# A slot of the second network: both first-layer products first, then the three tiles of its predecessor

## The chip, the cores and the metric

The kernel runs on one core of a Trainium2 chip. The metric is the time of one execution on the device, in microseconds (us). The engines are TensorE (PE, with its weight loads shown as PEld), VectorE (DVE), ScalarE (ACT), GpSimd (POOL) and SyncE (SP, which issues the transfers).

## The reference, cut to what matters

```python
def reference(**kwargs):
    attn_out = _attn_ref(q, k, v, p)             # packed attention, two softmaxes
    x = attn_out as 2304 tokens x 512
    x = _moe_ref(x, w_gate, w1, w2)              # eight experts, balanced gate
    return _moe2_ref(x, w_in, w_out, s, b)

def _moe2_ref(x, w_in, w_out, s, b):             # the second network
    h = x @ w_in                                 # 2304 x 512 @ 512 x 2048
    r = np.maximum(h, 0.0)
    g = s * (r * r) + b
    return (g @ w_out).astype(np.float32)        # 2304 x 2048 @ 2048 x 512
```

## The kernel before, in words

The program has three stages: attention, the experts, and the second network. Only the third is touched by the change. Every product is made of three passes (high x high, high x low, low x high), because each operand is held as a high part and a low part.

The second network goes through eight units `v` of 256 hidden columns (two halves `f` of 128), and within a unit through six blocks `b` of 384 tokens. One unit and one block make a **slot**, 48 in all. A slot has two first-layer products, here called f0 and f1 (`mm1b`, 12 matmuls of 384 columns each, L415), and three second-layer tiles t0, t1, t2 (`tile2`, 6 matmuls of 512 columns each, L390). The tiles of a slot are those of the slot before it: `coming` collects a slot's tiles, and `slot` hands them to the next slot as `ready`.

After f0 or f1 the result goes through an **epilogue**: ACT takes the positive part into `r` (L421), DVE multiplies into `g` (L422), which is the last reader of the product's PSUM bank, DVE scales and shifts `g` (L423), ACT casts it to the high part of `h` (L424), POOL subtracts to get the low part (L425). After a tile, DVE adds the PSUM bank to `acc` (L432; in unit 0 ACT copies instead, L430). In a tile, matmuls 1 to 3 read the f0 half of `h`, matmuls 4 and 5 the high part of its f1 half and matmul 6 the low part of its f1 half.

Buffers: the first-layer products share two PSUM banks (`ps_h`), the tiles three (`ps_y`). `r` is one buffer, `g` two. `h` holds three blocks.

Beside that, units 0 to 6 convert the next unit's weights from 64-bit words (`load_w64`): eight steps per unit, two per slot from block 1 on, given to `slot` as its `side` jobs. A step is seven DVE instructions (L111, L113, L114, L116, L118, L119, L120), one on ACT (L123) and one on POOL (L124). Every other step also issues a transfer of raw words on SP. The step's tiles `ex` and `m` are one buffer each, and a unit's first steps write weight buffers that the tiles of the slot before block 1 still read.

Order of the work: the attention stage is ordered by hand. After it, the framework's planner sets each engine's queue. It takes the program's order as priority and its own costs for when an instruction will be ready, so DVE's queue can hold a conversion step's instructions between those of an epilogue. Each queue is then carried out strictly in that order. The order in which a slot's jobs are written is set in `slot`:

```python
        per = [first[0]] + todo[:1] + [first[1]] + todo[1:]
        for n, job in enumerate(per):
            job()
            if side:
                side.pop(0)()
```

`first` holds f0 and f1, `todo` the predecessor's three tiles. A side job is written after each of them as long as there are any. `slot1` (the experts) and `slot2` (the second network) both call `slot`.

Of the kernel before, what the change touches and what calls it, by code (L numbers as in the profile page):

```python
# [15 lines left out]
B, H, S, HD, NPK = 4, 8, 576, 64, 32  # L16
NT, D = B * S, H * HD
E, FF1, FF2 = 8, 1024, 2048
NTT = NT // 128      # token tiles
NC = D // 128        # 128-row chunks of the model dimension  # L20
FU = 256             # hidden columns of a unit
UF = FU // 128
U1 = E * FF1 // FU   # units of the experts
UE = FF1 // FU       # units of an expert
U2 = FF2 // FU       # units of the second network
HB = S // 2          # tokens of a block of the experts: half a sequence
PT = 2 * S           # tokens of a pair of sequences
BLK = 384            # tokens of a block of the second network
NB = NT // BLK
TPB = BLK // 128  # L30
KC, NKC = 96, 6      # keys of a chunk, chunks
SCALE = 1.0 / 8.0    # 1 / sqrt(HD)
EPS = 1e-9
PASSES = ((0, 0), (0, 1), (1, 0))

# [2 lines left out]
def tile_kernel(ctx: ExitStack, tc: tile.TileContext, qT, kT, vv, pb, w1c, w2c, wcat64, wg, sv, bv, out):  # L38
# [8 lines left out]
    ps_h = pool("ps_h", 2, space=bass.MemoryType.PSUM)  # L47
    ps_m = pool("ps_m", 3, space=bass.MemoryType.PSUM)

    # chunks 0 and 1 of (high part, low part) of what the feed-forward networks read, by tokens:  # L50
    # first the second attention's weights, heads x packed keys in rows; then the experts' sum
    xa = [big.tile([128, 2, NT], F32R, name=f"xa{n}") for n in range(2)]
    xb = []
    acc = big.tile([128, NTT, D], F32, name="acc")
    h = big.tile([128, UF, 2, PT], F32R, name="h")

    ident = const.tile([128, 128], F32, name="ident")
    ones = const.tile([128, 128], F32, name="ones")
    wgr = const.tile([128, NC, E], F32, name="wgr")
    lg = const.tile([128, NTT, E], F32, name="lg")  # L60
    pm = const.tile([128, NTT, E], F32, name="pm")
    sb_ = const.tile([128, 2], F32, name="sb_")
# [6 lines left out]
    def x_part(n, c):  # L69
        return xa[n][:, c, :] if c < 2 else xb[n][:, c - 2, :]  # L70

# [1 line left out]
    wts = {}  # L73
    tmp_p = []

# [2 lines left out]
        return wts[key]  # L78

    def load_w1(u):  # L80
        # a head's rows: high parts in rows 0-63, low parts in rows 64-127
        w = w_new((1, u))
        for i in range(2):
            r = raw_p.tile([128, 1024], F32, tag="raw", name="raw")
            for n in range(2):
                nc.sync.dma_start(out=r[64 * n:64 * n + 64, :], in_=w1c[u, :, 1024 * i:1024 * i + 1024])
            yield
            A.copy(w[:, i, :], r)  # L88
            G.tensor_tensor(out=w[64:128, i, :], in0=r[64:128, :], in1=w[64:128, i, :].bitcast(F32),  # L89
                            op=ALU.subtract)  # L90
# [7 lines left out]
        G.tensor_tensor(out=w[:, 1, :], in0=r, in1=w[:, 0, :].bitcast(F32), op=ALU.subtract)  # L98

    def load_w64(key, f):  # L100
        # float64 words to float32: (mantissa + 2^20) * (sign, exponent - 20), rounded to nearest
        w = w_new(key)
        for half in range(2):
            r = raw_p.tile([128, 1024], U32, tag="raw", name="raw64")
            nc.sync.dma_start(out=r, in_=wcat64[f, :, 1024 * half:1024 * half + 1024])
            for q in range(2):
                rv = r[:, 512 * q:512 * q + 512].rearrange("p (n k) -> p n k", k=2)
                lo, hi = rv[:, :, 0], rv[:, :, 1]
                ex = tmp_p[-1].tile([128, 256], U32, tag="ex", name="ex")
                m = tmp_p[-1].tile([128, 256], F32, tag="m", name="m")  # L110
                V.tensor_scalar(out=ex, in0=hi, scalar1=20, scalar2=0x7FF,  # L111
                                op0=ALU.logical_shift_right, op1=ALU.bitwise_and)
                V.tensor_scalar(out=ex, in0=ex, scalar1=916.0, scalar2=1171.0, op0=ALU.max, op1=ALU.min)  # L113
                V.tensor_scalar(out=ex, in0=ex, scalar1=916.0, scalar2=8388608.0,  # L114
                                op0=ALU.subtract, op1=ALU.mult)
                V.scalar_tensor_tensor(out=ex, in0=hi, scalar=0x80000000, in1=ex,  # L116
                                       op0=ALU.bitwise_and, op1=ALU.bitwise_or)
                V.tensor_scalar(out=hi, in0=hi, scalar1=0xFFFFF, scalar2=None, op0=ALU.bitwise_and)  # L118
                V.scalar_tensor_tensor(out=m, in0=lo, scalar=2.0 ** -32, in1=hi, op0=ALU.mult, op1=ALU.add)  # L119
                V.scalar_tensor_tensor(out=m, in0=m, scalar=2.0 ** 20, in1=ex.bitcast(F32),  # L120
                                       op0=ALU.add, op1=ALU.mult)
                o = slice(512 * half + 256 * q, 512 * half + 256 * q + 256)
                A.copy(w[:, 0, o], m)  # L123
                G.tensor_tensor(out=w[:, 1, o], in0=m, in1=w[:, 0, o].bitcast(F32), op=ALU.subtract)  # L124
                yield

# [1 line left out]
    NG = B * 2  # L128
    at = {}

# [3 lines left out]
    accf = acc.rearrange("p t d -> p (t d)")  # L134

    def spare(o, n):
        # rows of acc, which the experts reach after the attention
        return accf[:, o:o + n]

    def a_load(g):  # L140
# [64 lines left out]
        at[g]["w"] = w  # L205

    def ppt(g):
        # a head's packed values, transposed, in rows 0-63 and again in rows 64-127
        b, i = divmod(g, 2)
        p_ = psa("h", "ps_p")  # L210
        nc.tensor.transpose(p_[:, :128], at[g].pop("w").rearrange("p a d -> p (a d)"), ident)
        pv = p_[:, :128].rearrange("p (c j n) -> p c j n", c=2, j=2)
        for j in range(2):
            r, o = slice(64 * j, 64 * j + 64), NPK * (j ^ (b & 1))
            A.copy(ppf[r, b, 2 * i:2 * i + 2, o:o + NPK], pv[r, :, j, :])
        s_ = [p_[:, NPK * n:NPK * n + NPK] for n in range(4)]
        o = [[pp[:, i, n, k, b ^ n, :] for n in range(4)] for k in range(2)]
        for n in range(4):
            A.copy(o[0][n], s_[n])  # L219
        for n in range(4):  # L220
            V.tensor_tensor(out=o[1][n], in0=s_[n], in1=o[0][n].bitcast(F32), op=ALU.subtract)
# [38 lines left out]
        A.copy(xa[0][o], a2T)  # L260
        G.tensor_tensor(out=xa[1][o], in0=a2T, in1=xa[0][o].bitcast(F32), op=ALU.subtract)

    # (stage, waves after the group's first)
    STAGES = ((sub2, 5), (norm2, 6), (s1, 0), (a1t, 1), (exp1, 0), (exp2, 5), (a2t, 7), (a2x, 7), (av, 2),
              (s2, 4), (ppt, 3))

# [2 lines left out]
            if 0 <= w - lag < NG:  # L269
                stage(w - lag)  # L270

# [1 line left out]
    def balance(mid):  # L273
        wgz = mid.tile([128, B, 2, 128], F32R, tag="wgz", name="wgz")
        G.memset(wgz.bitcast(F32), 0.0)
# [58 lines left out]
            V.scalar_tensor_tensor(out=pm, in0=pm, scalar=float(NT // E),  # L334
                                   in1=c[:, 2].to_broadcast([128, NTT, E]), op0=ALU.mult, op1=ALU.mult)

# [1 line left out]
    zs = {}  # L338

    def zmm(u, n, p_=None):  # L340
        # rows of a head in a sequence: block (head ^ sequence) of 32, so that blocks stay where they are
        i, k = divmod(n, 2)
        if n == 0:
            for pr in range(2):
                zs[u, pr] = z_p.tile([128, 2, 2, 2, FU], F32R, tag="z", name="z")
        w = wts[1, u].rearrange("p a m -> p (a m)")
        p_ = psm("ps_z") if p_ is None else p_
        for j in range(2):
            m = 2 * k + j
            for a in range(2):  # L350
                mmul(p_[:, j * FU:(j + 1) * FU], pp[:, i, m, a].rearrange("p q n -> p (q n)"),  # L351
                     w[:, (4 * i + m) * FU:(4 * i + m + 1) * FU], start=(a == 0), stop=(a == 1))
        return p_
# [50 lines left out]
                                       op0=ALU.mult, op1=ALU.add)  # L404
        return put

# [1 line left out]
    def mm1b(v, b, f):  # L408
        w = wts[3, v, f]
        p_ = ps_h.tile([128, 512], F32, tag="h", name="ps_1")  # L410
# [31 lines left out]
        A.copy(xh, p_[:, :BLK])  # L442
        V.tensor_tensor(out=xl, in0=p_[:, :BLK], in1=xh.bitcast(F32), op=ALU.subtract)

# [1 line left out]
    order = [(u, pr) for u in range(U1) for pr in range(2)]  # L446
    ready, coming = [], []

    def slot(first, side=()):
        # the products of a block, among them what earlier blocks made ready  # L450
        side = list(side)
        todo = ready[:]
        del ready[:]
        per = [first[0]] + todo[:1] + [first[1]] + todo[1:]
        for n, job in enumerate(per):
            job()
            if side:
                side.pop(0)()
        for s_ in side:
            s_()  # L460
        ready.extend(coming)
        del coming[:]
# [9 lines left out]
    def slot2(v, b, side=()):  # L472
        first = [lambda f=f: mm1b(v, b, f) for f in range(UF)]
        ws = [[wts[3, v, f][:, k, D:2 * D] for k in range(2)] for f in range(UF)]
        for t in range(TPB):
            coming.append(lambda t=t: tile2(ws, (b % 3) * BLK + t * 128, b * TPB + t, put2(v)))
        slot(first, side)

    def side1(x, q):
        jobs = []  # L480
# [14 lines left out]
    with tc.tile_pool(name="early", bufs=1) as early:  # L495
        pp = early.tile([128, 2, 4, 2, B, NPK], F32R, name="pp")
        ppf = early.tile([128, B, NC, 2 * NPK], F32, name="ppf")
        with tc.manual_schedule(), tc.tile_pool(name="at", bufs=1) as at_p:
# [26 lines left out]
            for q in range(4):  # L525
                side = [lambda: wave(NG + 3 + q), lambda: next(loads, None)]
# [6 lines left out]
        with tc.tile_pool(name="mid", bufs=1) as mid:  # L533
# [3 lines left out]
            for x in range(1, len(order) - 1):  # L537
                for q in range(4):
                    side = side1(x, q)
# [17 lines left out]
    with tc.tile_pool(name="late", bufs=1) as late:  # L557
        tmp_p.append(late)
        xb += [late.tile([128, 2, NT], F32R, name=f"xb{n}") for n in range(2)]
        x = len(order) - 1  # L560
        for q in range(4):
            slot1(x, q, [lambda b=q - 1, c=c: flip(b, c) for c in range(NC)] if q else ())
        for v in range(U2):
            conv = None
            for b in range(NB):
                side = []
# [53 lines left out]
```

## Time and profile before

| what | value |
| --- | --- |
| median of 3 runs | 1840.36 us (1840.31 to 1841.12) |
| span of the profiled execution, first to last instruction | 1839.9 us |
| time beyond the span, by the median | 0.5 us |
| PE busy, of the span | 1761.9 us (96%) |
| DVE busy, of the span | 1399.3 us (76%) |
| mean granted TensorE clock | 0.990 |
| second network, first product to the last instruction | 1396.3 to 1839.9 us |

The profiled execution has no time of its own apart from its span; the span and the median of the runs differ by 0.5 us. A share of the whole span is a mean over stages that differ, so the second network has to be read slot by slot. In the rows, `[0.80 <-ACT h L424]` means that the engine was idle for 0.80 us before the instruction and that the write of `h` by ACT at line 424 ended the idle time.

### The profile page before, as it was taken

The numbers are of one execution on the slowest core, as the hardware profiler recorded it, in microseconds if no ns is written. First come the engines' busy times: TensorE is split into PE (matmuls) and PEld (weight loads), VectorE is DVE, ScalarE is ACT, GpSimd is POOL, SyncE is SP. The second block draws the span as 40 slices with busy tenths as digits, with TensorE's granted clock in tenths as the row PEclk, the third lists the DMA queues.
The fourth block names the chain that finished last, engine by engine and source line by source line (L and its number), as shares of the span: only waits on it lengthen the run. The fifth ranks groups of instructions, "written<-read, shape, count | busy, mean of one in ns | idle before, by whom it ended". The sixth has DMA issues, their size and how long they took to land.

```text
span 1839.9 us, 26426 instructions
## 1 busy us (share of the span) xinstructions
PE 1761.9 (96%) x9797; PEld 1519.7 (83%) x9797; DVE 1399.3 (76%) x2828; ACT 809.2 (44%) x1845; POOL 410.1 (22%) x288
## 2 busy tenths in 40 slices
PE   5789999999999999999999999999999999999999
PEld 2478888888888888888888888888888978888888
DVE  2757978777777777777777787777999489888874
ACT  3574475445444444544444454444434422222222
POOL 2541112111112211111221111121112233333332
PEclk9799999999999999999999999999999999999999
DMA  9421111111111111111111111111011011111102
GB/s 247 131 58 46 35 36 49 44 35 35 46 35 35 56 37 35 35 46 35 35 58 35 35 35 46 35 35 58 24 35 46 12 35 46 47 35 35 35 12 103
DMA packets 30225, 88.23 MB, mean 48 GB/s; under 512 B 4240, under 2 KB 9360, under 8 KB 30096
## 3 DMA queue, kind: packets, MB, share of 16 engines
q1 hardware_dynamic: 30096, 86.54, 16.2%
q8 instruction: 77, 1.26, 0.3%
q14 instruction: 52, 0.43, 0.1%
HBM read 81.81 MB, written 4.72 MB: 47 GB/s over the span
## 4 chain that ended last, share of the span: by engine, by line
PE 63%; DVE 20%; ACT 6%; issue 5%; POOL 2%; DMA 2%; SPq 0%; ACTq 0%; POOLq 0%; DVEq 0%
PE ps L390 37%; PE ps L378 18%; DVE z L371 6%; ACT z L369 5%; PE ps L415 5%; PE ps_z L351 2%; DVE m L120 2%; DVE ex L114 2%; DVE acc L403 1%; POOL h L425 1%; DVE m L119 1%; DVE acc L432 1%; DVE g L422 1%; DVE ex L116 1%; DVE ex L111 1%
## 5 line engine op out<-in xcount | busy, mean ns | idle before, releaser
L390 PE MATMUL ps<-w,h 128*128 128x512 f32 x4320 | 1119.3, 396 | 33.8 <-ACT h L424 9.4
L390 PEld LDWEIGHTS ps<-w,h 128*128 128x128 f32 x4320 | 778.5, 188 | 200.9 <-DVE h L382 19.9
L378 PEld LDWEIGHTS ps<-xa,z 128*128 128x128 f32 x3072 | 465.4, 189 | 46.6 <-ACT z L369 3.4
L378 PE MATMUL ps<-xa,z 128*128 128x288 f32 x3072 | 495.9, 297 | 4.9 <-ACT z L369 3.0
L403 DVE SCALAR_TENSOR_TENSOR acc<-ps,pm,acc 128x512 f32<-128x512 f32 x504 | 374.1, 747 | 109.3 <-PE ps L390 107.9
L381 ACT ACTIVATE h<-ps 128x288 fp32r<-128x288 f32 x512 | 210.7, 411 | 555.8 <-PE ps L378 502.3
L371 DVE TENSOR_TENSOR z<-ps_z,z 32x256 fp32r<-32x256 f32 (+1 forms) x768 | 370.3, 506 | 39.3 <-ACT z L369 33.8
L382 DVE SCALAR_TENSOR_TENSOR h<-ps,h 128x288 fp32r<-128x288 f32 x512 | 232.6, 454 | 128.1 <-ACT h L381 121.3
L369 ACT CAST z<-ps_z 32x256 fp32r<-32x256 f32 (+1 forms) x768 | 310.2, 434 | 18.2 <-PE ps_z L351 7.2
L89 POOL TENSOR_TENSOR w<-raw,w 64x1024 fp32r<-64x1024 f32 x64 | 152.6, 2405 | 414.9 <-issue 378.7
L98 POOL TENSOR_TENSOR w<-raw,w 128x1024 fp32r<-128x1024 f32 x32 | 76.9, 2402 | 596.4 <-ACT w L97 560.2
L425 POOL TENSOR_TENSOR h<-g,h 128x384 fp32r<-128x384 f32 x96 | 100.9, 1051 | 249.2 <-ACT h L424 247.2
L415 PE MATMUL ps<-xa,w 128*128 128x384 f32 x576 | 147.5, 337 | 0.0
L415 PE MATMUL ps<-xb,w 128*128 128x384 f32 x576 | 147.1, 336 | 0.0
L424 ACT CAST h<-g 128x384 fp32r<-128x384 f32 x96 | 49.4, 514 | 161.2 <-DVE g L423 161.1
L422 DVE SCALAR_TENSOR_TENSOR g<-ps,r 128x384 f32<-128x384 f32 x96 | 53.0, 552 | 77.1 <-ACT r L421 75.7
L415 PEld LDWEIGHTS ps<-xa,w 128*128 128x128 f32 x576 | 105.6, 188 | 6.7
L415 PEld LDWEIGHTS ps<-xb,w 128*128 128x128 f32 x576 | 104.7, 188 | 0.0
L88 ACT CAST w<-raw 128x1024 fp32r<-128x1024 f32 x64 | 67.0, 1047 | 67.1 <-PE ps L390 63.0
L432 DVE TENSOR_TENSOR acc<-ps,acc 128x512 f32<-128x512 f32 x126 | 86.0, 684 | 9.2 <-PE ps L390 9.0
L351 PE MATMUL ps_z<-w,pp 128*128 128x256 f32 x512 | 82.4, 283 | 0.7 <-ACT pp L219 0.5
L124 POOL TENSOR_TENSOR w<-m,w 128x256 fp32r<-128x256 f32 x64 | 48.1, 751 | 127.0 <-ACT w L123 127.0
(108 smaller groups left out, 776.9 us busy)
## 6 DMA issues: line engine op xcount, KB each, us to landing
raw<-w1c SPq DMA_DIRECT2D x128, 256.0 KB, 3.9
raw<-w2c SPq DMA_DIRECT2D x32, 512.0 KB, 3.4
raw<-wcat SPq DMA_DIRECT2D x32, 512.0 KB, 3.4
acc<-kT SPq DMA_DIRECT2D x8, 576.0 KB, 9.6
acc<-vv SPq DMA_DIRECT2D x8, 576.0 KB, 10.5
out<-acc SPq DMA_DIRECT2D x18, 256.0 KB, 2.0
q__224<-qT SPq DMA_DIRECT2D x1, 576.0 KB, 10.2
q__299<-qT SPq DMA_DIRECT2D x1, 576.0 KB, 14.8
```

The lines of the kernel that those rows point to most:

```text
L89: G.tensor_tensor(out=w[64:128, i, :], in0=r[64:128, :], in1=w[64:128, i, :].bitcast(F32), op=ALU.subtract)
L351: mmul(p_[:, j * FU:(j + 1) * FU], pp[:, i, m, a].rearrange("p q n -> p (q n)"), w[:, (4 * i + m) * FU:(4 * i + m + 1) * FU], start=(a == ...
L369: A.copy(o[:, 0], i_)
L371: V.tensor_tensor(out=o[:, 1], in0=i_, in1=o[:, 0].bitcast(F32), op=ALU.subtract)
L378: mmul(p_[:, :HB], z[:, a, q // 2, i, f * 128:(f + 1) * 128], xa[k][:, i, t], start=(n + i == 0), stop=(n + i == 3))
L381: A.activation(out=hh, in_=p_[:, :HB], func=AF.Relu)
L382: V.scalar_tensor_tensor(out=hl, in0=p_[:, :HB], scalar=0.0, in1=hh.bitcast(F32), op0=ALU.max, op1=ALU.subtract)
L390: mmul(y, h[:, f, a, hc:hc + 128], ws[f][k], start=(n == 0), stop=(n == 3 * UF - 1))
L403: V.scalar_tensor_tensor(out=a, in0=y, scalar=pm[:, T, u // UE:u // UE + 1], in1=a, op0=ALU.mult, op1=ALU.add)
L415: mmul(p, w[:, a, c * 128:(c + 1) * 128], x_part(k, c)[:, b * BLK:(b + 1) * BLK], start=(n == 0), stop=(n == 3 * NC - 1))
L425: G.tensor_tensor(out=hl, in0=g, in1=hh.bitcast(F32), op=ALU.subtract)
L432: V.tensor_tensor(out=a, in0=y, in1=a, op=ALU.add)
```

## The change

In `slot`, an argument `apart` chooses the order of the jobs. The experts keep theirs. The second network passes `apart=False`: a slot is then written as f0, f1, t0, t1, t2, where it was f0, t0, f1, t1, t2. The side jobs are still written after the first, second, ... job, so the second one now follows f1 and not t0. Nothing is added or removed. (The diff also deletes comments.)

```diff
-    def slot(first, side=()):
-        # the products of a block, among them what earlier blocks made ready
+    def slot(first, side=(), apart=True):
+
         side = list(side)
         todo = ready[:]
         del ready[:]
-        per = [first[0]] + todo[:1] + [first[1]] + todo[1:]
+        per = [first[0]] + todo[:1] + [first[1]] + todo[1:] if apart else first + todo
...
-        slot(first, side)
+        slot(first, side, apart=False)
```

## Rows read from the trace of the kernel before

**Rows 1.** The page: busy time of each engine over the span.
```profile
PE 1761.9 (96%) x9797; PEld 1519.7 (83%) x9797; DVE 1399.3 (76%) x2828; ACT 809.2 (44%) x1845; POOL 410.1 (22%) x288
```

**Rows 2.** Stretches, block 1 to block 1: units 1, 2, and five slots of 6.
```profile
1462.35:1517.72 55.37, 52.06 (x253) 44.81 (x252) 45.60 (x97) 14.96 (x34) 18.89 (x21) 1.00 0.12 39
1517.72:1572.42 54.70, 51.87 (x254) 44.90 (x252) 46.89 (x98) 14.32 (x33) 18.61 (x21) 1.00 0.12 39
...
1736.49:1781.98 45.49, 43.15 (x211) 37.50 (x210) 37.97 (x79) 12.21 (x28) 16.36 (x19) 1.00 0.07 23
```

**Rows 3.** Stretches: blocks 1 to 5 of unit 2, then block 0.
```profile
1517.72:1526.07 8.35, 8.35 (x44) 7.57 (x43) 7.14 (x16) 2.19 (x6) 3.76 (x5) 1.00 0.19 63
...
1526.07:1534.75 8.68, 8.60 (x43) 7.49 (x42) 8.47 (x19) 1.83 (x4) 3.06 (x4) 1.00 0.18 60
1534.75:1544.81 10.06, 8.90 (x43) 7.43 (x42) 9.75 (x22) 2.63 (x6) 3.64 (x5) 1.00 0.15 54
1544.81:1554.86 10.05, 8.92 (x44) 7.43 (x42) 9.74 (x22) 3.01 (x7) 3.63 (x5) 1.00 0.17 54
1554.86:1564.08 9.22, 8.77 (x44) 7.41 (x42) 7.81 (x16) 2.43 (x5) 2.49 (x4) 1.00 0.00 0
1564.08:1572.42 8.34, 8.34 (x44) 7.57 (x42) 3.97 (x7) 2.24 (x5) 2.04 (x3) 1.00 0.01 3
```

In Rows 2 and 3 the columns are: the stretch, its length, then busy time (and instructions) of PE, PEld, DVE, ACT, POOL, then the granted clock, the DMA share and GB/s.

**Rows 4.** Timeline of PE: block 3 of unit 2, then block 0.
```profile
1536.86 0.86 PE L390 MATMUL ps<-w,h 128*128 128x512 f32 x3
1538.52 0.73 PE L390 MATMUL ps<-w,h 128*128 128x512 f32 x2 [0.80 <-ACT h L424]
1539.61 0.50 PE L390 MATMUL ps<-w,h 128*128 128x512 f32 x1 [0.36 <-POOL h L425]
...
1564.08 0.51 PE L415 MATMUL ps<-xa,w 128*128 128x384 f32 x2
...
1566.18 1.55 PE L390 MATMUL ps<-w,h 128*128 128x512 f32 x6
1567.57 0.51 PE L415 MATMUL ps<-xa,w 128*128 128x384 f32 x2
...
1569.66 2.92 PE L390 MATMUL ps<-w,h 128*128 128x512 f32 x12
```

**Rows 5.** Who waited for whom in the second network: total, times, longest.
```profile
PE ps L390 <- ACT h L424: 9.4, 13, 0.8
...
PE ps L390 <- POOL h L425: 7.1, 18, 0.5
```

**Rows 6.** Timeline of DVE, unit 2: L422 of f0 in blocks 2, 3, 4; of f1 in 4.
```profile
1532.05 0.55 DVE L422 SCALAR_TENSOR_TENSOR g<-ps,r 128x384 f32<-128x384 f32 x1
...
1542.08 0.55 DVE L422 SCALAR_TENSOR_TENSOR g<-ps,r 128x384 f32<-128x384 f32 x1
...
1552.11 0.55 DVE L422 SCALAR_TENSOR_TENSOR g<-ps,r 128x384 f32<-128x384 f32 x1
...
1555.91 0.55 DVE L422 SCALAR_TENSOR_TENSOR g<-ps,r 128x384 f32<-128x384 f32 x1
```

**Rows 7.** Timelines of POOL and DVE, unit 2: an L425 and the L120 beside it.
```profile
1533.87 1.12 POOL L425 TENSOR_TENSOR h<-g,h 128x384 fp32r<-128x384 f32 x1 [2.35 <-ACT h L424]
...
1534.15 1.12 DVE L120 SCALAR_TENSOR_TENSOR m<-m,ex 128x256 f32<-128x256 f32 x1
```

**Rows 8.** Lines L114, L120, one unit: minimum, median, maximum in ns.
```profile
L114 DVE TENSOR_SCALAR ex<-ex x9: 283/709/720, 1525.9 to 1580.6; 128x256 uint32<-128x256 uint32 x9
...
L120 DVE SCALAR_TENSOR_TENSOR m<-m,ex x8: 424/772/1124, 1529.8 to 1578.8; 128x256 f32<-128x256 f32 x8
```

**Rows 9.** Groups by line and shape over one unit (1526.07 to 1580.76 us).
```profile
L425 POOL TENSOR_TENSOR h<-g,h 128x384 fp32r<-128x384 f32 x12 | 12.8, 1063 | 28.5 <-ACT h L424 28.5
...
L424 ACT CAST h<-g 128x384 fp32r<-128x384 f32 x12 | 6.2, 514 | 23.6 <-DVE g L423 23.6
L421 ACT ACTIVATE r<-ps 128x384 f32<-128x384 f32 x12 | 5.8, 488 | 4.2 <-PE ps L415 4.2
```

## The prediction

> **What bounds the kernel now.** I read the page first: PE is busy for 96% of the span and DVE for 76% [rows 1]. That says little of one stage, so the next view is that of stretches, cut at the starts of slots. In block 0 of a unit a slot takes 8.34 us and PE is busy all of it; that is what PE alone needs. Blocks 2 to 5 of the same unit take 8.68, 10.06, 10.05 and 9.22 us [rows 3]. Their PE work is the same, so 38.01 - 4 x 8.34 = 4.65 us of a unit are waiting. The DVE column explains where they sit: in block 0 DVE is busy 3.97 us, in blocks 2 to 4 it is busy 8.47 of 8.68, 9.75 of 10.06 and 9.74 of 10.05 us. DVE is full there because it converts weights as well.
>
> The timeline of PE shows at which instruction the waiting falls: after the third matmul of t0 (until ACT has written the high part) and before its sixth (until POOL has written the low part) [rows 4]. These read the f1 half of `h` from the slot before. The waits view confirms that hardly anything else stops PE's matmuls in this stage [rows 5]; the idle times it lists are smaller than the loss, since a matmul that comes after a wait overlaps nothing, so I take the loss from slot lengths.
>
> Over the stage: unit 1 loses 55.37 - 6 x 8.34 = 5.33 us, unit 2 54.70 - 50.04 = 4.66 us; units 3 to 5 repeat unit 2 to 0.01 us; unit 6 loses 45.49 - 5 x 8.34 = 3.79 us [rows 2]. Units 0 and 7 have no such wait. The sum is 5.33 + 4 x 4.65 + 3.79 = 27.7 us, the most that moving the tiles can return.
>
> **The change part by part.** It moves t0 behind f1. PE's work is the same: f0 takes 1566.18 - 1564.08 = 2.10 us, t0 1.39, f1 2.09, t1 with t2 2.76 [rows 4], in either order 8.34. No instruction, transfer or wait is added. The raw-word transfers are issued by the side job behind f0, which stays; the second side job moves behind f1, and neither queue of SP or POOL has anything else to be passed in these slots. Where no conversion runs (unit 7, blocks 3 to 5 of unit 0, block 0), no product waits today, and I cost the edit at nothing: PE's own 8.34 us hide it.
>
> *Room of the f1 half.* Before, f1's end is followed by t1 and t2 (2.76), the next f0 (2.10) and five matmuls of t0 (1.15) until the low part is wanted: 6.0 us. From the end of L422 to the end of the low part takes 1533.87 + 1.12 - (1532.05 + 0.55) = 2.4 us [rows 6, 7]. So DVE may finish L422 at most 3.6 us after f1 without a stall. After, three tiles (4.15), f0 and f1 (4.19) and five matmuls lie between: 9.5 us, less 2.4 makes 7.1 us.
>
> *What is late next.* A product's PSUM bank is wanted again by the same product of the next slot, 8.34 - 2.10 = 6.24 us after its end, and L422 is its last reader. That holds in both orders, and it is tighter than 7.1. So the room of L422 grows from 3.6 to 6.24 us, not to 7.1.
>
> *How late DVE would be if PE never stalled.* DVE has next to no idle time from block 2 to the start of block 5, so its times there do not depend on PE's stalls. Block 2's f0 ends at 1526.07 + 2.10 = 1528.17; without stalls the later ones end at 1536.51 and 1544.85. Their L422 end at 1532.60, 1542.63 and 1552.66 [rows 6]: 4.4, 6.1 and 7.8 us late, 1.7 more each slot (DVE's 10.03 against PE's 8.34). For f1 of block 4, which would end at 1517.72 + 3 x 8.34 + 5.58 = 1548.32, L422 ends at 1556.46: 8.1 us. Less the room before, 8.1 - 3.6 = 4.5 us of stall, and the slots show 4.65: the account holds. With the room after, f0 stalls 7.8 - 6.24 = 1.6 and f1 in all 8.1 - 6.24 = 1.9 us per unit. I assume that the planner sends L422 of f1 forward with f1.
>
> *DVE's own pace.* The traces do not show how the planner will interleave the queue, and it matters, because POOL delays DVE. L120 started 0.28 us after an L425 and took 1.12 us, ending 0.28 us after it; alone it takes 0.42 [rows 7, 8]. L114 mostly takes 0.71 instead of 0.28 [rows 8], beside L124. In one slot that is 0.70 + 2 x 0.43 = 1.56 us out of POOL's 3.64. After, no tile's addition stands between f0's epilogue and a conversion step, and one instead of two behind f1's, so f1's L425 may hit a conversion too (+0.70); the additions that stand free then may shield an L124 each (-0.86). Between these bounds I take +0.1 us per slot, near zero because gains and losses come from the same two rows. Over the three slots in which lateness builds up that is 0.3 us: residue 2.2 us per unit.
>
> Here the Trainium skill has a rule that speaks against the change ("SBUF — State Buffer", section "Who interferes with whom"): a DVE instruction with two SBUF inputs, or in a two-port mode, and a GpSimd instruction exclude each other, and the loser waits out the whole of the other. The rows above agree in kind. By the rule's worst alignment all 3.64 us of POOL would be charged; that is the third rival.
>
> *Sum.* The residue is 2.2 us in units 2 to 5; unit 1 loses 0.7 more and unit 6 0.9 less, as now: 2.9 + 8.8 + 1.3 = 13.0 us. Returned: 27.7 - 13.0 = 14.7. Span 1839.9 - 14.7 = 1825.2; the median lies 0.5 above the span, so 1825.7, say **1826 us**, 0.8% faster.
>
> **The rivals.**
>
> *All of the waiting goes.* If the additions shield POOL's instructions so that DVE needs 0.6 us less per slot, f1's lateness is 8.1 - 1.86 = 6.24 and nothing stalls: 1839.9 - 27.7 + 0.5 = 1812.7 us. For it: 1.56 us per slot is lost to POOL now. Against: with each collision gained another may open.
>
> *The pace of DVE eats the gain.* The residue is 1.9 us plus three times the added time per slot; it reaches today's 4.65 at +0.93 us. At that price the time is the old one, 1840, and the wait has moved from t0 to the start of f0 and f1.
>
> *POOL holds DVE in full (slower).* If every POOL instruction met a conversion, a slot would cost 3.64 - 1.56 = 2.1 us more; the residue would be 1.9 + 6.3 = 8.2 us, 3.5 more than now in each of six units: +21, 1861 us. It decides from +0.93 us per slot; half-way, at 1.5, it gives 1.9 + 4.5 = 6.4 us, +10.5 in all, 1851. Against: additions and epilogue instructions read PSUM or lie between, and some always will.
>
> *One buffer `r` (slower).* f1 now ends 2.09 us behind f0, not 3.48. L421 of f1 must wait until f0's L422 has read `r`, and on ACT it may stand behind f0's L424. If L422 of f1 then follows f0's L423 directly on DVE, DVE idles for L424 and L421, 0.51 + 0.49 [rows 9], with the hand-overs about 1.2 us per slot; above 0.93, so the residue is 1.9 + 3.6 = 5.5 and the time +5, 1845 us. Against: DVE's queue has conversion instructions to put between, as it has now.
>
> *It does not do what it says.* The planner orders the queues itself. If PE's queue keeps a tile between the products, or DVE's queue keeps f1's epilogue where it was in spite of the earlier product, L422 of f1 is 8.1 + 1.4 = 9.5 us late, and 9.5 - 6.24 = 3.3 us of residue leave about 1832; with an unchanged PE order it is 1840.
>
> **How the numbers follow.** Two times within 0.2% (3.7 us) are about what a measurement of this kernel can't tell apart. Forecast, 1818 to 1836 us (+0.93 us per slot excluded, some shielding included): 0.57. All of the waiting gone, 1812 to 1818: 0.20. The gain eaten, by DVE's pace or an unchanged order, 1837 to 1844: 0.13. POOL in full, 1844 to 1861: 0.05. One `r`, 1844 to 1848: 0.05. The first two are faster: 0.77. The third is no change: 0.13. The last two are slower: 0.10. The range 1812 to 1840 us takes in the first two and the nearer part of the third, and leaves out about 0.15; it is as wide as DVE's unknown pace makes it.
>
> **What the profile after would show.** PE: 24 matmuls at L415 in a row and then 18 at L390 in each slot; no idle time before the fourth and sixth matmul of t0; stalls, if any, before the first matmul of f0 or f1, released by DVE's L422. Slots: blocks 2 and 3 at 8.34 to 8.7, the residue in blocks 4 and 5. DVE: still nearly full in blocks 2 to 4, busy time per slot within 0.3 us of now for the same work; L114 and L120 with other medians. Unit 7 and block 0 unchanged at 8.34.
>
> The prediction would be wrong if DVE's work per slot rose by 0.9 us or more (third and fourth rival), if L422 of f1 stood in DVE's queue where it stands now, or if the loss of these slots came from something else than lateness of L422, so that the longer room bought nothing.

## The result, and the profile after

The changed kernel takes 1819.47 us (median of 4 runs, 1816.04 to 1820.18) against 1840.34 us, a ratio of 0.988 with a 95% interval of 0.987 to 0.989. The forecast was 1826 us in a range of 1812 to 1840. In a second series the same program took 1817.07 us against 1843.56, ratio 0.985 (0.984 to 0.986). The profiled execution has a span of 1814.3 us. It is the fastest of its four runs (1816.04 us), so the spans differ by 25.6 us where the medians differ by 20.9.

The page, first section, has PE at 97% in place of 96% [rows 1]:

```profile
PE 1751.9 (97%) x9797; PEld 1522.9 (84%) x9797; DVE 1392.6 (77%) x2828; ACT 806.9 (44%) x1845; POOL 408.7 (23%) x288
```

Stretches of the profile after: unit 1 and unit 2 from block 1 to the next block 1, and five slots of unit 6; then blocks 1 to 5 of unit 2 and the block 0 behind them (columns as in [rows 2, 3]).

```profile
1461.06:1513.29 52.23, 50.58 (x253) 44.98 (x252) 46.54 (x97) 14.68 (x33) 18.97 (x20) 1.00 0.13 41
1513.29:1563.74 50.45, 50.14 (x254) 45.36 (x252) 45.09 (x98) 13.98 (x32) 18.17 (x20) 1.00 0.13 43
1715.00:1756.54 41.54, 41.54 (x212) 37.81 (x210) 36.57 (x79) 11.76 (x27) 16.11 (x18) 1.00 0.07 26
...
1513.29:1521.60 8.31, 8.31 (x44) 7.56 (x42) 7.87 (x18) 2.61 (x6) 3.29 (x5) 1.00 0.19 63
1521.60:1529.90 8.30, 8.30 (x43) 7.57 (x42) 8.03 (x19) 2.00 (x5) 3.43 (x4) 1.00 0.19 63
1529.90:1538.21 8.31, 8.31 (x43) 7.56 (x42) 8.04 (x20) 2.31 (x6) 2.23 (x4) 1.00 0.22 67
1538.21:1546.52 8.31, 8.31 (x44) 7.56 (x42) 8.11 (x19) 1.51 (x4) 3.12 (x4) 1.00 0.19 63
1546.52:1555.43 8.91, 8.60 (x43) 7.54 (x42) 7.64 (x17) 2.72 (x6) 3.04 (x3) 1.00 0.00 0
1555.43:1563.74 8.31, 8.31 (x44) 7.56 (x42) 5.42 (x10) 2.83 (x6) 3.06 (x3) 1.00 0.01 3
```

Blocks 2, 3 and 4, which took 8.68, 10.06 and 10.05 us [rows 3], now take what PE alone needs. One short wait of 0.60 us is left in block 5. Unit 2 loses 50.45 - 6 x 8.31 = 0.6 us where it lost 4.66 [rows 2], unit 1 loses 52.23 - 49.84 = 2.4 in place of 5.3. In unit 6 no wait is left: its five slots take 41.54 us, that is 5 x 8.31. Units 3 to 5 repeat unit 2. What is left over the stage is 2.4 + 4 x 0.6 = 4.8 us, of 27.7.

Timeline of PE, unit 2, where the short wait is:

```profile
1547.93 0.51 PE L415 MATMUL ps<-xa,w 128*128 128x384 f32 x2
...
1549.10 0.61 PE L415 MATMUL ps<-xa,w 128*128 128x384 f32 x2 [0.31 <-DVE g L422]
```

and the waits of PE over the stage after the transposes (waiter, releaser, total, times, longest):

```profile
PE ps L415 <- DVE g L422: 2.8, 6, 1.4
```

The waits of t0 for the high and low part of `h` [rows 4, 5] are gone. The wait that took their place stands before f1 (before f0 in unit 1) and ends with L422, the last reader of the product's bank.

The account of the two profiled spans, 1839.9 - 1814.3 = 25.6 us: 22.9 us of waiting in units 1 to 6; 1.7 us because every one of the 48 slots is 0.035 us shorter (8.34 to 8.31), which nothing in the prediction had (it took 8.34 us for either order); and about 1 us because the second network began earlier (1395.4 against 1396.3 us), before anything changed. That start lies between 1393.6 and 1398.4 us in the profiles of this study, so totals of single executions can't be compared to better than some 5 us, and the slots are compared instead.

### The profile page after: what moved, and what is told of

Same layout as the page of the kernel before. It is cut to its first block, busy times and chain, and to the rows that moved or that the text cites. A ratio compares the mean times of both kernels' runs of the same rounds, so it can differ in the third digit from the quotient of the medians.

```text
span 1814.3 us, 26426 instructions
## 1 busy us (share of the span) xinstructions
PE 1751.9 (97%) x9797; PEld 1522.9 (84%) x9797; DVE 1392.6 (77%) x2828; ACT 806.9 (44%) x1845; POOL 408.7 (23%) x288
## 4 chain that ended last, share of the span: by engine, by line
PE 66%; DVE 21%; ACT 6%; issue 4%; DMA 3%; POOL 1%; SPq 0%; DVEq 0%; ACTq 0%; POOLq 0%
PE ps L390 40%; PE ps L378 18%; DVE z L371 7%; PE ps L415 6%; ACT z L369 5%; PE ps_z L351 2%; DVE acc L403 1%; DVE ex L111 1%; DVE acc L432 1%; DVE ex L116 1%; DVE m L119 1%; DVE ex L114 1%; DVE g L422 1%; DVE m L120 1%; DVE ex L113 1%
## 5 line engine op out<-in xcount | busy, mean ns | idle before, releaser
L390 PE MATMUL ps<-w,h 128*128 128x512 f32 x4320 | 1102.1, 395 | 16.8 <-DVE h L382 5.0
L415 PE MATMUL ps<-xa,w 128*128 128x384 f32 x576 | 147.9, 337 | 2.8 <-DVE g L422 2.8
L415 PE MATMUL ps<-xb,w 128*128 128x384 f32 x576 | 147.0, 336 | 0.0
L425 POOL TENSOR_TENSOR h<-g,h 128x384 fp32r<-128x384 f32 x96 | 98.6, 1027 | 201.7 <-ACT h L424 201.6
L424 ACT CAST h<-g 128x384 fp32r<-128x384 f32 x96 | 49.3, 514 | 149.2 <-DVE g L423 149.2
L415 PEld LDWEIGHTS ps<-xa,w 128*128 128x128 f32 x576 | 104.4, 188 | 8.6 <-DVE g L422 5.1
L415 PEld LDWEIGHTS ps<-xb,w 128*128 128x128 f32 x576 | 104.5, 188 | 0.0
L422 DVE SCALAR_TENSOR_TENSOR g<-ps,r 128x384 f32<-128x384 f32 x96 | 53.0, 552 | 59.0 <-ACT r L421 59.0
L432 DVE TENSOR_TENSOR acc<-ps,acc 128x512 f32<-128x512 f32 x126 | 85.0, 683 | 14.0 <-PE ps L390 14.0
L124 POOL TENSOR_TENSOR w<-m,w 128x256 fp32r<-128x256 f32 x64 | 49.2, 769 | 150.0 <-ACT w L123 150.0
```

What stands on the lines that cost most here:

```text
L390: mmul(y, h[:, f, a, hc:hc + 128], ws[f][k], start=(n == 0), stop=(n == 3 * UF - 1))
L415: mmul(p, w[:, a, c * 128:(c + 1) * 128], x_part(k, c)[:, b * BLK:(b + 1) * BLK], start=(n == 0), stop=(n == 3 * NC - 1))
L425: G.tensor_tensor(out=hl, in0=g, in1=hh.bitcast(F32), op=ALU.subtract)
L432: V.tensor_tensor(out=a, in0=y, in1=a, op=ALU.add)
```

## The experiments

**Again.** The changed kernel unaltered.

> The changed kernel once more, unaltered. Every theory expects the time of the first measurement, 1816 to 1821 us, and in the trace a wait of about 0.6 us in each of units 2 to 6 before f1, and of about 2.4 us in unit 1 before f0. It says how far two executions of the same program differ.

Measured: 1817.07 us (1814.83 to 1818.32). The waits are in the same places: unit 1 has slots of 8.69 and 10.21 us, units 2 to 5 one of 8.87 each. Unit 6, where the expectation had one too, has none.

**The two parts of the edit apart.** The edit moves a tile and, with it, the second conversion step of a slot. Both kernels here hold that step back by one job.

```diff
+        late = second and len(side) <= 2
...
-            if side:
+            if side and not (late and n == 1):
                 side.pop(0)()
```

`second` is set for the second network; the limit of two side jobs leaves out the slots of unit 0 that transpose. One kernel has this with the tiles in the old order, so the second step stands behind f1; the other has it with `apart=False`, so the step stands behind t0.

> One part alone: t0 stays between f0 and f1 as before the change, and only the second conversion step of a slot is written behind f1 instead of t0. Theory (room): t0 still wants the f1 half after the same time, so the waits before its fourth and sixth matmul stay: 1836 to 1844 us, by what DVE's new interleaving costs or saves. Rival (the moved conversion step made the gain, by letting L422 of f1 go first): 1818 to 1826 us.

> The other part alone: f0, f1, t0, t1, t2 as after the change, with the second conversion step of a slot written behind t0, as before it. Theory (room): the gain of the change but for DVE's interleaving, 1815 to 1826 us. Rival (the conversion step's place made the gain): 1840 us.

Measured: the step alone 1842.63 us, ratio 0.999 (0.998 to 1.000); the tile alone 1815.33 us, ratio 0.985 (0.982 to 0.988). In the profile of the step alone the old waits stand where they stood:

```profile
1539.57 0.73 PE L390 MATMUL ps<-w,h 128*128 128x512 f32 x2 [0.80 <-ACT h L424]
1540.66 0.50 PE L390 MATMUL ps<-w,h 128*128 128x512 f32 x1 [0.36 <-POOL h L425]
```

All of the gain belongs to the tile: with the tile alone every slot of units 1 to 6 is within 0.06 us of the changed kernel's.

**Without conversions.** Does the new order save TensorE something by itself? Both kernels leave out the conversions for units 1 to 7 and read the weights of unit 0 in every unit.

```diff
-        w = wts[3, v, f]
+        w = wts[3, 0, f]
...
-                if v + 1 < U2:
+                if False:
```

> The order of before, without the conversion of weights in units 0 to 6: every unit reads the weights of unit 0, so the output is another one, and seven eighths of the conversions and their transfers are left out. Theory (room): DVE is then nowhere late, no product waits, and the time is the floor, 1806 to 1813 us. Rival (the order of the products costs TensorE something by itself): well above the same kernel in the new order.

> The order of after, without the conversion of weights in units 0 to 6, as in the run beside it. Theory (room): the same floor within 3 us, of which 1.7 us is the slot's 8.31 us in place of 8.34 in the traces. Rival (the new order is worth about 20 us to TensorE by itself): some 1790 us.

Measured: 1810.18 and 1809.65 us, ratios to the kernel before 0.982 (0.980 to 0.984) and 0.982 (0.979 to 0.984), no difference that the runs can tell. No wait of PE is listed in either. One unit in each (order of before, then of after):

```profile
1464.57:1514.61 50.04, 50.04 (x253) 45.40 (x252) 23.80 (x42) 12.08 (x24) 12.20 (x13) 1.00 0.00 1
```

```profile
1468.46:1518.30 49.84, 49.84 (x254) 45.38 (x252) 24.36 (x42) 11.45 (x24) 12.22 (x12) 1.00 0.00 1
```

The order alone is worth 0.20 us a unit. The waits need the conversions; the order decides how much of their lateness PE sees.

**More between the products.** A third order puts two tiles between them, which shortens the room.

```diff
-        per = [first[0]] + todo[:1] + [first[1]] + todo[1:] if apart else first + todo
+        k = 1 if apart else 2
+        per = [first[0]] + todo[:k] + [first[1]] + todo[k:]
```

> A third order: f0, t0, t1, f1, t2. From f1's end to the sixth matmul of the next t0 lie one tile, f0 and five matmuls, 4.6 us, so L422 may end 2.2 us after f1, against 3.6 before the change. Theory (room): the loss per unit is L422's lateness of about 8 us less that, some 6 us in place of 4.65, so 1844 to 1854 us, with the waits at the same two matmuls of t0. Rival (only DVE's pace counts, not the distance): 1836 to 1844 us, no order in sight.

Measured: 1852.37 us, ratio 1.0055 (1.0036 to 1.0075). Unit 2 takes 56.91 us, 6.9 more than PE needs, and the waits are the same two, both longer than in [rows 4]:

```profile
1538.55 0.73 PE L390 MATMUL ps<-w,h 128*128 128x512 f32 x2 [1.16 <-ACT h L424]
1539.75 1.43 PE L390 MATMUL ps<-w,h 128*128 128x512 f32 x5 [0.47 <-POOL h L425]
```

So 2.2, 3.6 and 6.24 us of room give 6.9, 4.65 and 0.6 us of loss per unit. The theory had about 6, 4.5 and 1.9: the direction holds and so does the order of size; the last is discussed below.

**More PSUM banks.** f1's product goes to the pool of three banks.

```diff
-        p_ = ps_h.tile([128, 512], F32, tag="h", name="ps_1")
+        p_ = psm("ps_1") if f else ps_h.tile([128, 512], F32, tag="h", name="ps_1")
# bank_v1: "if f and v", so that unit 0 keeps the two banks
```

> The kernel before (tile between the products) with the same additional banks as in the other run. Theory (room): before the change the f1 half of h is wanted 3.6 us after the end of L422's room began, the bank only after 6.24, so banks change nothing: 1840 us. Rival (banks were the limit all along): 1815 to 1825 us.

> The changed kernel, with f1's product in the three PSUM banks of the third pool and f0's alone in its two; no queue changes its order. Theory (room): what is left of the waiting, 5.1 us over units 1 to 6, is a wait for the bank that L422 reads last, so it goes except about 1 us in unit 1, where L422 of f1 is 8.1 us late against 7.1 us until the low part of h is wanted: about 4 us less than the changed kernel, 1815. Rival (pace: DVE's new queue order alone made the gain and the banks don't matter): the changed kernel's time, 1819.

> The changed kernel with f1's product in the third pool's banks, as before, but from unit 1 on, where no transposes (flips) use that pool. No queue changes its order. Expected by the room theory: units 2 to 6 without waits (2.8 us less), unit 1 as it was, since there the tiles' banks, read last by the additions, stop PE by the same 2.4 us, and unit 0's slots as in the changed kernel: 1814 to 1816 us where the changed kernel has 1817 to 1819. Rival (sharing the pool was not what made block 2 of unit 0 longer by 1.55 us): that slot stays at 12.07 us.

Measured: in the old order 1844.36 us, ratio 1.0005 (0.9993 to 1.0016): nothing. In the new order 1814.42 us (0.9838, 0.9823 to 0.9853), and from unit 1 on 1814.37 us (0.9839, 0.9823 to 0.9854); the changed kernel in the series of the first had 1817.07. These intervals overlap, so the total does not settle it; the slots do. Units 1 and 2 from unit 1 on:

```profile
1463.75:1515.99 52.24, 50.89 (x253) 45.05 (x252) 46.52 (x97) 14.66 (x33) 18.97 (x20) 1.00 0.12 41
1515.99:1565.83 49.84, 49.84 (x253) 45.38 (x252) 45.07 (x98) 13.97 (x32) 18.13 (x20) 1.00 0.12 43
```

Unit 2 has lost its last 0.6 us: the bank was its limit. Unit 1 keeps its 2.4 us, but for another reason, the tiles' own banks, which the additions read last:

```profile
1494.83 3.05 PE L390 MATMUL ps<-w,h 128*128 128x512 f32 x12 [0.24 <-DVE acc L432]
...
1502.92 1.62 PE L390 MATMUL ps<-w,h 128*128 128x512 f32 x6 [0.86 <-DVE acc L432]
```

The first of the two runs expected only 1 us to stay in unit 1, by the next limit on `h`; the additions came before it. The third expectation's rival was that the shared pool doesn't lengthen block 2 of unit 0. That slot took 11.59 us in the third run, 12.07 with the shared pool and 10.51 in the changed kernel; but with the old order and no bank moved (the step alone) it took 11.69 against 10.10. What differs is the granted clock of the slot: 0.86 in both bank runs and 0.85 in the step alone, 1.00 in the changed kernel and in the kernel before. That part was not a matter of banks.

**DVE's pace, slower.** Each conversion step for units 1 to 7 repeats one mask, which changes no value.

```diff
                 V.tensor_scalar(out=hi, in0=hi, scalar1=0xFFFFF, scalar2=None, op0=ALU.bitwise_and)
+                if key[1]:
+                    V.tensor_scalar(out=hi, in0=hi, scalar1=0xFFFFF, scalar2=None, op0=ALU.bitwise_and)
```

> The changed kernel with one more DVE instruction in each conversion step for units 1 to 7 (the mask of L118 is applied twice, which leaves the values as they are): 0.33 us a step, 0.66 us a slot by L118's pitch in the trace. Theory (room and pace): lateness of f1's L422 in block 4 grows by three slots' worth, 2 us, from 6.7 to 8.7 us against 6.2 us of room, so each of units 1 to 6 waits about 2 us longer: 12 us more than the changed kernel, 1825 to 1838 us. Rival (what is left of the waiting has nothing to do with DVE's pace): 1816 to 1821 us.

Measured: 1826.84 us (1825.61 to 1830.26), ratio 0.992 (0.990 to 0.993), 7 to 10 us more than the changed kernel. Unit 2 takes 52.91 us, 2.5 more than the 50.45 above (2 were expected), and both products wait for their bank (the added lines move L415 to L417 and L422 to L424):

```profile
1550.49 0.62 PE L417 MATMUL ps<-xa,w 128*128 128x384 f32 x2 [0.96 <-DVE g L424]
...
1554.17 0.62 PE L417 MATMUL ps<-xa,w 128*128 128x384 f32 x2 [1.31 <-DVE g L424]
```

L422 of f1 in block 4 is 8.7 us late, as expected, but it gets there by another way than 0.66 us more in each slot: in blocks 1 to 4 of unit 2 it is 0.85, 0.77, 0.57 and 2.2 us later than in the changed kernel, so most arises in block 4. Unit 1 even loses less, 1.8 us in place of 2.4, and units 1 to 6 together lose 10.7 us more, where 12 were expected. The run shows that DVE's queue sets what is left; it does not bear out the sum slot by slot.

**DVE's pace, faster.** The scaling of `g` goes to ACT, in the old order and in the new.

```diff
-        V.tensor_scalar(out=g, in0=g, scalar1=sb_[:, 0:1], scalar2=sb_[:, 1:2], op0=ALU.mult, op1=ALU.add)
+        A.activation(out=g, in_=g, func=AF.Identity, scale=sb_[:, 0:1], bias=sb_[:, 1:2])
```

> The order of before, with the scaling and shifting of g (L423) moved from DVE to ACT, so that DVE has 0.8 to 0.9 us less to do in a slot. Theory (room and pace): the loss per unit is lateness less 3.6 us of room; lateness falls by three slots' worth, 2.5 us or more, so the loss falls from 4.65 to some 2 us a unit, 1821 to 1830 us, with the waits still before the fourth and sixth matmul of t0. Rival (only the order of the products counts, and DVE's pace is without effect): 1840 us.

> The changed kernel with L423 on ACT as well. Theory (room and pace): f1's L422 in block 4 is then less than 6.2 us late in every unit, unit 1 too, so no product and no tile waits in units 1 to 6 and 5 us go: 1811 to 1815 us; unit 0's flips may gain or lose a microsecond, since ACT serves them as well. Rival (ACT's queue becomes the next wait, since L423 and L424 then both stand on it ahead of the next L421): 1817 us or more, with waits for ACT in PE's rows.

Measured: 1842.23 us in the old order, ratio 0.9993 (0.9984 to 1.0002); 1824.96 us in the new, ratio 0.990 (0.989 to 0.991), that is 5 to 8 us slower than the changed kernel. Both expectations of the theory failed. The times are those that the rivals gave (1840 us, and 1817 or more), but the second rival's sign, waits for ACT among PE's, is absent, since PE waits for L422:

```profile
PE ps L415 <- DVE g L422: 6.8, 11, 1.2
```

The queue of DVE shows what I had left out. In unit 2 of the old order with the scaling on ACT, the first and the eighth L120 (the last DVE instruction of a step), and between them L422 of f0 in block 3:

```profile
1518.49 0.43 DVE L120 SCALAR_TENSOR_TENSOR m<-m,ex 128x256 f32<-128x256 f32 x1
...
1541.04 0.55 DVE L422 SCALAR_TENSOR_TENSOR g<-ps,r 128x384 f32<-128x384 f32 x1
...
1550.21 0.42 DVE L120 SCALAR_TENSOR_TENSOR m<-m,ex 128x256 f32<-128x256 f32 x1
```

The same two L120 in the kernel before:

```profile
1519.78 0.43 DVE L120 SCALAR_TENSOR_TENSOR m<-m,ex 128x256 f32<-128x256 f32 x1
...
1554.22 1.12 DVE L120 SCALAR_TENSOR_TENSOR m<-m,ex 128x256 f32<-128x256 f32 x1
```

A step now takes 31.72 / 7 = 4.5 us in place of 34.44 / 7 = 4.9. The time that the epilogue gave back was filled with conversion, so DVE is full for a shorter stretch, but within it L422 is as late as before: it ends 25.3 us after the start of block 1 here (1541.59 - 1516.28), 24.9 before (1542.63 - 1517.72) [rows 6]. The count shows the filling: from L422 of f0 in block 1 of unit 2 to that in block 4, DVE carries out 42 conversion instructions, six steps, in the kernels before and after, and 48 (old order) and 47 (new order) with the scaling on ACT. Nearly a whole seventh step stands where the six scalings stood. That the planner fills whatever time it believes DVE to have is how I read it; its costs were not looked into, so why it does so is not shown.

Why the new order even loses 5 to 8 us by it, the filling alone doesn't say. From one L422 of f0 to the next, in blocks 1 to 4 of unit 2, DVE's instructions together take 1.8, 2.2 and 2.3 us longer than the same lines do when no POOL instruction lies beside them, where the changed kernel has 1.5 each time; L422 of f0 comes 10.03 to 10.53 us apart in place of 9.61, and the unit loses 1.9 us in place of 0.6. A small part is the second rival's mechanism after all, one step removed: L422 of f1 in block 4 waits for an L421 that stands behind L423 and L424 in ACT's queue, and the product that waits for this L422 costs some 0.3 of the 1.9 us.

```profile
1552.30 0.56 DVE L422 SCALAR_TENSOR_TENSOR g<-ps,r 128x384 f32<-128x384 f32 x1 [0.79 <-ACT r L421]
```

On ACT, L423 takes 0.71 us in place of 0.48, which lengthens the way to `h`. In the old order one slot each of units 2, 3, 4 and 6 has a granted clock of about 0.86 as well (in unit 2 the slot of 12.24 us, which has waits of 1.04 and 0.86 us in it). That is not what undid the gain: units 1 and 5, at 1.00 throughout, lose 4.55 and 4.20 us, only 0.8 and 0.45 less than before.

## Why the prediction was right

*The bound.* Right. The waits of t0 for the f1 half were the loss: they vanish with the tile moved, stay with only the step moved, and are not there without conversions.

*The most to be had, 27.7 us.* Right: without conversions the old order takes 1810.2 us, 31.8 less than the kernel before in its series (1842.0). Of that, 3.6 us belong to block 1 of unit 0, where the transposes wait for DVE and which then takes 10.57 us in place of 14.19; some 28 are left.

*The room, 3.6 to 6.24 us.* Right. The new limit is the product's bank, as predicted: more banks do nothing in the old order and remove the last wait of units 2 to 5 in the new. L422 of f1 did go forward with f1, as assumed: it starts 2.9 us behind that of f0 (1529.29 - 1526.37), where it was 4.55. That the tiles' banks follow next was not foreseen.

*DVE's own pace.* This is the term that was mis-sized. I took +0.1 us a slot; it was -0.42 in unit 2. L422 of f0 in blocks 1 to 4 of the profile after, then of f1 in block 4:

```profile
1516.76 0.55 DVE L422 SCALAR_TENSOR_TENSOR g<-ps,r 128x384 f32<-128x384 f32 x1
...
1526.37 0.55 DVE L422 SCALAR_TENSOR_TENSOR g<-ps,r 128x384 f32<-128x384 f32 x1
...
1535.98 0.55 DVE L422 SCALAR_TENSOR_TENSOR g<-ps,r 128x384 f32<-128x384 f32 x1
...
1545.59 0.55 DVE L422 SCALAR_TENSOR_TENSOR g<-ps,r 128x384 f32<-128x384 f32 x1
...
1548.50 0.55 DVE L422 SCALAR_TENSOR_TENSOR g<-ps,r 128x384 f32<-128x384 f32 x1
```

Those of f0 come every 9.61 us, not 10.03. f1 of block 4 ended at 1513.29 + 3 x 8.31 + 4.18 = 1542.40 and its L422 at 1549.05: 6.65 us late. Less 6.2 us of room that is 0.4, and the slot shows 0.6. With the pace as it was, the same sum had given 1.9. The reason for the new pace is in POOL's and DVE's timelines, first before, an L124 and the L114 beside it:

```profile
1535.79 0.74 POOL L124 TENSOR_TENSOR w<-m,w 128x256 fp32r<-128x256 f32 x1 [0.80 <-ACT w L123]
```

```profile
1535.97 0.71 DVE L114 TENSOR_SCALAR ex<-ex 128x256 uint32<-128x256 uint32 x1
```

and after:

```profile
1528.19 1.02 POOL L425 TENSOR_TENSOR h<-g,h 128x384 fp32r<-128x384 f32 x1 [2.35 <-ACT h L424]
1529.17 0.80 POOL L124 TENSOR_TENSOR w<-m,w 128x256 fp32r<-128x256 f32 x1
```

```profile
1528.34 1.03 DVE L111 TENSOR_SCALAR ex<-raw 128x256 uint32<-128x256 uint32 x1
1529.29 0.55 DVE L422 SCALAR_TENSOR_TENSOR g<-ps,r 128x384 f32<-128x384 f32 x1
1529.76 0.36 DVE L113 TENSOR_SCALAR ex<-ex 128x256 uint32<-128x256 uint32 x1
```

An L425 and an L124 run back to back here. One instruction waits for the first (1.03 us in place of 0.29), and the second falls under L422 and costs L113 only 0.07. Before, an L425 and an L124 each met a conversion instruction of their own, at +0.70 and +0.43 us [rows 7, 8]. Added up over all the instructions from one L422 of f0 to the next, 21 in each kernel, DVE takes 1.8 us longer than undisturbed before and 1.5 after; that is 0.3 of the 0.42 us. (The prediction had 1.56 before; it left out an L119 at +0.24.) The Trainium skill has a rule for the single meeting ("SBUF — State Buffer", "Who interferes with whom": whichever of the two comes second is blocked while the first has the shared ports). The trace agrees in kind: L111 ends at 1529.37, 0.16 us behind the L425 beside it; in which of DVE's modes L111 runs, no run shows. That POOL would meet DVE more often, which I feared from the rule, did not happen in unit 2.

Unit 1 is the test within the same trace. There DVE's queue is interleaved otherwise, and L422 of f0 in blocks 2 and 3 come 10.21 us apart:

```profile
1475.57 0.55 DVE L422 SCALAR_TENSOR_TENSOR g<-ps,r 128x384 f32<-128x384 f32 x1
...
1485.78 0.55 DVE L422 SCALAR_TENSOR_TENSOR g<-ps,r 128x384 f32<-128x384 f32 x1
```

Three slots at 10.21 in place of 9.61 make 1.8 us; unit 1 loses 2.4 and unit 2 0.6. There DVE takes 2.0 us a slot longer than undisturbed, 0.5 more than in unit 2, which is most of the 0.6 us between the two paces. So most of the change in pace goes with where the planner's queue happens to meet POOL: it came out better in units 2 to 6 and worse in unit 1 (10.02 us before), and nothing in the trace before told which. For the residue the sum was 13.0 us and the trace has 4.8; that, and the 1.7 us of PE, are the difference between the forecast's 14.7 us and the profile's 25.6, with 1 us of earlier start. A small term was off the other way: the prediction set the time 0.5 us above the span, and in the runs after it each time lies about 1.8 us above its own span.

So the mechanism and the range held and the forecast itself was 6.5 us too high. That the time fell into the forecast's own case was in part luck: 1819.47 us lies 1.5 us inside its lower edge of 1818, and the second series, 1817.07 us, lies in the case where all of the waiting goes. Of what the profile was to show, one more thing missed: DVE's busy time fell by 0.4 us a slot (over three slots from 29.2 us of 30.1 to 28.0 of 28.8), where 0.3 was the most allowed.

*The rivals.* All of the waiting gone needed 0.6 us of DVE's time a slot; 0.42 came, and 22.9 of the 27.7 us went. No POOL in full, no gain eaten. PE's queue has both products ahead of the tiles in every slot, so the edit does what it says. One buffer `r` cost nothing visible while conversions run: between L423 of f0 and L422 of f1 DVE has conversion instructions. In blocks 5 and 0 of unit 2, where it has none, DVE idles 1.1 us for L421, and no product waits for what follows.

## What to carry to other kernels

Where a queue is full for a stretch, measure by how much the instruction that releases PE will be late at the end of that stretch, and compare it with the distance until its result is wanted: the loss is about the difference, and a consumer moved back by a few microseconds removed most of it here without a single instruction less. Then name the next limit (here the product's bank, then the tile's bank), since the room ends there. Taking work from the full engine was no substitute here, because the freed time was filled with other work ahead of the urgent instruction. And don't read an order's effect on DVE from its amount of work alone: the same instructions took 9.61 or 10.21 us a slot, by what they met on POOL.

## What the runs showed of the hardware

The clock of TensorE can fall inside the second network. In unit 0, PE waits 2.0 us for the transposes' bank; behind that wait the stretch of 3.3 us has a granted clock of 0.51 in one execution (bank run from unit 1 on, first line), that is the level of 1.2 GHz, and the whole slot behind the same wait has 1.00 in the changed kernel (second line):

```profile
1418.94:1422.23 3.29, 3.29 (x13) 3.19 (x12) 2.56 (x7) 1.26 (x3) 0.73 (x1) 0.51 0.48 159
```

```profile
1417.32:1427.83 10.51, 10.31 (x60) 9.05 (x58) 9.99 (x23) 5.80 (x13) 3.03 (x3) 1.00 0.17 50
```

Unit 0 is written alike in both, so the same work got either clock. The fall costs about 1.1 to 1.6 us of that slot (11.59 and 12.07 us in the two bank runs against 10.51), which is one reason why totals a few microseconds apart were not read as effects.

In the kernels before and after, VectorE is held up beside GpSimd alone: from block 1 of unit 1 to the start of unit 7, every DVE instruction that takes over 0.1 us more than its line does undisturbed (86 before, 72 after) overlaps a POOL instruction and ends 0.15 to 0.28 us after it. L422 and L432, which read PSUM, keep to 0.54 to 0.56 and 0.68 to 0.69 us there, whatever POOL does.

The 24 matmuls of 384 columns and 18 of 512 of a slot take 8.31 us in two blocks and 8.34 in four, without conversions too. What in the turn from one kind to the other costs this, no run separates.
